# One 32 KB run per partition for K and V, and a softmax per head: a decode layer on one core

## The chip, the cores and the metric

The kernel runs on one core of a Trainium2 chip. The metric is the device time of one execution in microseconds (us), as the median of several runs. An execution has a *span*, from the first to the last instruction of the profile, and a little time around it. The engines are PE (matmuls; PEld is its loading of weights), DVE (vector work), ACT (activations), POOL (general work) and SP (which here only issues transfers). Sixteen DMA engines move data between HBM and the on-chip SBUF. PE writes its results to PSUM, eight banks of 2 KB in each partition.

## The reference

One decode step of a layer that mixes two branches with a gate. Eight batches, one new token each, width 576. Branch A is attention with 32 query heads over 16 K/V heads of 128, over the last 2048 of 8192 cached positions; branch B is an MLP of width 4608.

```python
W = min(4096, max(256, Sk // 4))                     # 2048
q = (x @ wq).reshape(B, Sq, Hq, Dh).transpose(0, 2, 1, 3)
k = jnp.repeat(k_cache[:, :, Sk - W:, :], rep, axis=1)   # rep = 2
v = jnp.repeat(v_cache[:, :, Sk - W:, :], rep, axis=1)
scores = jnp.einsum("bhqd,bhkd->bhqk", q, k) * (Dh ** -0.5)
p = _softmax(scores, axis=-1)
o = jnp.einsum("bhqk,bhkd->bhqd", p, v)
a = o.transpose(0, 2, 1, 3).reshape(B, Sq, Hq * Dh) @ wo
b = _gelu(_layernorm(x) @ w1 + b1) @ w2 + b2
g = _sigmoid((x * gate_w).sum(-1, keepdims=True))
return g * a + (1 - g) * b
```

All tensors are bf16. One K/V head of all batches is 8 x 2048 x 128 x 2 bytes = 4 MB of K and as much of V, so K and V are 134 MB of the 154 MB that are moved.

## The kernel before

**Transfers.** SP issues nearly all of them, in one order: wq and w1 first, then a stream of items, then w2. `K i` and `V i` are the 4 MB of head i; `W` is a quarter of wo, after each fourth V. The stream is K0, K1, K2, V0, K3, V1, K4, and so on: K runs three heads ahead of V. K and V go through four slots of 64 KB in each partition, taken in turn, so an item takes the slot of the item four places before it. SP waits until that slot is free: for a K item when its four transposes are done, for a V item when its PV matmuls are done. A load is cut into 256 runs of 16 KB (32 key blocks of 64 keys, by 8 batches); a partition holds two of them, of two batches.

**K.** A head is four *halves* (two units, i = 2 head + u, of two halves each). For each half DVE transposes 128x2048 words (`tr`, line 647, about 2.3 us) into one of two KT buffers, and PE multiplies it in eight matmuls of 512 columns (`qk`, line 659 for the first of four and line 175 for the three that keep the weights). The transposes of a KT buffer wait for the `qk` two halves earlier. The scores of two heads (a *group*, eight halves) add up in PSUM banks 0 to 3; a mask written into the banks beforehand keeps the parts that a partition doesn't own out of the maximum.

**Softmax of a group.** In this order: `mx` (DVE, line 620) takes the maximum over the 2048 scores of each partition; `mq`, a small matmul on PE and `nb` (lines 621 to 623) combine the partitions; `exp` (ACT, line 624) writes P and its sums; `mask` (ACT, line 629) fills the banks for the next group, and the first `qk` of that group waits for it; `pt` (DVE, line 631) transposes P into one of two buffers; a small matmul adds the sums (line 633) and `rc` (line 635) inverts them. POOL copies the queries of the next group into place in four instructions (line 614).

**V.** `pv` (PE, line 681) is 32 matmuls a head: 16 key steps, two column tiles of 32 columns side by side. After the second head of a group come `vmul` and `acc` (DVE, lines 691 and 694), `ew` (POOL, line 696), `us` (PE, line 700), `oev` (ACT, line 703), and after four heads `oT` (DVE, line 706); then a projection adds the product with that quarter of wo to a PSUM bank (line 563). The products with w2 are added to the same bank at the end.

**Order.** A planner goes through all the operations with a cost for each, a transfer rate of 428 GB/s and 1.8 us of latency, and takes, among those whose predecessors are placed, the one that can start first, a priority counting 0.2 us a step (the softmax has priority 5, mask 4, `vmul` to `us` 6, `oev` and `oT` 9, `tr`, `qk` and `pv` 0):

```python
est = max(eng_free[op.eng], r)
key = (est - 0.2 * op.prio, -op.prio, i)
```

What comes out is a fixed order on each engine; on the chip an instruction waits only for those that it depends on and for those ahead of it on its engine. Ties go to the operation that was added first, in the order of the stream.

Of the kernel before, what the change touches and what calls it, by code (L numbers as in the profile page):

```python
# [181 lines left out]
def build_kernel(nc, A_x, A_k_cache, A_v_cache, A_wq, A_wo, B_x, B_w1, B_b1, B_w2, B_b2, gate_w, out):  # L182
# [9 lines left out]
    HG = 2  # L192
    NG = Hkv // HG
    ND = 4
    SE = 4 * W
# [14 lines left out]
    with ExitStack() as es:  # L210
# [19 lines left out]
        req("i32", 32, F32)  # L230
        req("iqm", 32, F32)
        req("maskr", 4, F32)
        req("maskq", 4, F32)
        req("maskv", 4, F32)
        req("kq", 128, F32)
        req("selv", 128, F32)
        req("seln", 128, F32)
# [10 lines left out]
        req("qbd", 4 * 4 * 128, BF)  # L248
# [7 lines left out]
        req("sm", 32 * NG, F32)  # L256
        req("gcol", 1, F32)
        req("rr", 2, F32)
# [3 lines left out]
        req("oT", NG * 128, BF)  # L262
# [41 lines left out]
        i32 = view("i32")  # L304
# [3 lines left out]
        iqm, maskr, selv = view("iqm"), view("maskr"), view("selv")  # L308
# [7 lines left out]
        qbd = view("qbd").rearrange("p (u h m) -> p u h m", u=4, h=4)  # L316
# [13 lines left out]
        oT = view("oT").rearrange("p (i j c) -> p i j c", i=NG // 2, j=WOR)  # L330
        seln = view("seln")
# [53 lines left out]
        o_mR = add("pool", lambda e: e.affine_select(out=maskR, in_=ones_bf, pattern=[[0, 128], [1, 4]], compare_op=ALU.is_equal,  # L385
                                                     fill=0.0, base=0, channel_multiplier=-1), deps=[o_ones], name="maskR", cost=0.8, prio=-1)
        o_mL = add("pool", lambda e: e.affine_select(out=maskL, in_=zeros_bf, pattern=[[0, 16], [1, 4], [0, 2]], compare_op=ALU.is_equal,
# [70 lines left out]
        o_i32 = [add("dve", lambda e: e.tensor_reduce(out=i32, in_=ident.rearrange("p (q m) -> p m q", q=4), axis=AXL.X, op=ALU.add), deps=[o_ident, o_obl], name="i32", cost=0.3, prio=-1)]  # L458
        o_iqm = add("dve", lambda e: e.tensor_reduce(out=iqm.rearrange("p (q m) -> p q m", q=4), in_=ident.rearrange("p (q r m) -> p q m r", q=4, r=4), axis=AXL.X, op=ALU.add), deps=[o_ident, o_obl], name="iqm", cost=0.3, prio=-1)
        o_maskr = add("dve", lambda e: e.tensor_reduce(out=maskr, in_=i32.rearrange("p (r m) -> p r m", r=4), axis=AXL.X, op=ALU.add), deps=o_i32, name="maskr", cost=0.2, prio=-1)  # L460
        o_maskq = add("dve", lambda e: e.tensor_reduce(out=maskq, in_=ident.rearrange("p (q m) -> p q m", q=4), axis=AXL.X, op=ALU.add), deps=[o_ident, o_xT], name="maskq", cost=0.3)
        o_kq = add("pool", lambda e: e.tensor_copy(kq.rearrange("p (q m) -> p q m", q=4), bass.AP(arena_f, offset=foffs("i32"), ap=[[AST // 2, 128], [0, 4], [1, 32]])), deps=o_i32, name="kq", cost=0.3, prio=-1)
        o_maskhd = add("dve", lambda e: e.tensor_reduce(out=maskhd, in_=iqm.rearrange("p (n h) -> p h n", h=2), axis=AXL.X, op=ALU.add), deps=[o_iqm], name="maskhd", cost=0.2, prio=-1)

        def seln_fn(e):
            dst = bass.AP(arena_f, offset=foffs("seln"), ap=[[AST // 2, 128], [32, 4], [8, 4], [1, 8]])
            src = bass.AP(arena_f, offset=foffs("i32"), ap=[[AST // 2, 128], [8, 4], [0, 4], [1, 8]])
            return e.tensor_copy(dst, src)
        o_seln = [add("pool", seln_fn, deps=o_i32, name="seln", cost=0.3, prio=-1)]
        o_selv = []  # L470
        for l in range(4):
            def selv_fn(e, l=l):
                dst = bass.AP(arena_f, offset=foffs("selv") + 32 * l, ap=[[AST // 2, 128], [1, 2], [8, 4], [2, 4]])
                s0, s1 = [bass.AP(arena_f, offset=foffs("iqm") + 16 * (l % 2) + h, ap=[[AST // 2, 128], [8, 2], [0, 4], [2, 4]]) for h in range(2)]
                return e.tensor_tensor(out=dst, in0=s0, in1=s1, op=ALU.add)
            o_selv.append(add("pool", selv_fn, deps=[o_iqm], name="selv%d" % l, cost=0.3, prio=-1))
# [39 lines left out]
        for he in range(4):  # L516
            for u in range(2):
                def fn(e, he=he, u=u):
                    src = bass.AP(ps, offset=BK_SEL * 512 + 8 * he + u, ap=[[PST, 128], [64, 16], [2, 4], [32, 2]])
                    return e.activation(out=q4[:, he, :].rearrange("p (l u b h) -> p l u b h", l=16, u=2, b=4)[:, :, u, :, :], in_=src, func=ACTF.Copy)  # L520
                o_q4.append(add("act", fn, deps=[o_selp], name="q4_%d_%d" % (he, u), cost=0.3))
# [78 lines left out]
        def load_item(cache, nm, hkv):  # L600
            s = take_slot()
            src = cache[:, hkv, S0:Sk, :].rearrange("b (x r) d -> x b (r d)", x=32)
            d = dma("sp", lambda e: e.dma_start(slot(s).rearrange("p (u n) -> p u n", u=2), src), "s%d" % s, 8 * W * Dh * 2, deps=slot_free[s], name="%s%d" % (nm, hkv), after=last_dma[-1:])
            last_dma.append(d)
            slot_free[s] = []
            return s, d

        def query(g):
            qb_done[g] = []
            for a in range(4):  # L610
                def fn(e, a=a):
                    dst = bass.AP(arena, offset=32 * a * AST + aoffs("qbd") + 32 * a, ap=[[AST, 32], [520, 4], [128, 4], [1, 8]])
                    src = bass.AP(arena, offset=32 * a * AST + aoffs("q4") + 32 * g, ap=[[AST, 32], [8, 4], [256, 4], [1, 8]])
                    return e.tensor_copy(dst, src)  # L614
                qb_done[g].append(add("pool", fn, deps=o_q4 + [o_qz, qk_unit.get(4 * g - 1)], name="qr%d_%d" % (g, a), cost=0.4))

        def softmax(g):
            k = lambda i, n=1, parts=128, p0=0: sm[p0:p0 + parts, g, i:i + n]
            MX, MXQ, NB, S = 0, 1, 7, 12
            mx = add("dve", lambda e: e.tensor_reduce(out=k(MX), in_=ps[:, 0:4, :].rearrange("p a n -> p (a n)"), axis=AXL.X, op=ALU.max), deps=[qk_unit[4 * g + 3]], name="mx%d" % g, cost=2.25, prio=5)  # L620
            mq = add("dve", lambda e: e.tensor_scalar(out=k(MXQ, 4), in0=maskq, scalar1=k(MX), scalar2=-SCALE, op0=ALU.mult, op1=ALU.mult), deps=[mx, o_maskq], name="mq%d" % g, cost=0.16, prio=5)
            gp = add("pe", lambda e: e.matmul(ps[:, BK_S, 4:8], kq, k(MXQ, 4), start=True, stop=True), deps=[mq, o_kq, o_u] + b6_r[-1:], after=b6_w[-1:], name="max_pe%d" % g, cost=0.5, prio=5)  # L622
            nb = add("dve", lambda e: e.tensor_reduce(out=k(NB), in_=ps[:, BK_S, 4:8], axis=AXL.X, op=ALU.min), deps=[gp], name="nb%d" % g, cost=0.16, prio=5)  # L623
# [3 lines left out]
            if g + 1 < NG:  # L627
                query(g + 1)
                mask_done[g + 1] = add("act", lambda e: e.activation(out=ps[:, 0:4, :].rearrange("p a (n c) -> p (a n) c", c=4), in_=bass.AP(arena_f, offset=foffs("maskv"), ap=[[AST // 2, 128], [0, 512], [1, 4]]), func=ACTF.Copy),  # L629
                                       deps=[ex] + qb_done[g + 1], name="mask%d" % (g + 1), cost=1.75, prio=4)  # L630
            pt_done[g] = add("dve", lambda e: e.transpose(bass.AP(arena, offset=aoffs("PT") + 2048 * (g % 2), ap=[[AST, 128], [8, 64], [512, 4], [1, 8]]), Pm.rearrange("p (r q m) -> p r q m", q=4, m=8)),  # L631
                             deps=[ex] + ([pv_last[g - 2]] if g >= 2 else [o_yTp, o_hT]), name="pt%d" % g, cost=2.4, prio=5)
            sp_ = add("pe", lambda e: e.matmul(ps[:, BK_S, 0:1], seln, k(S), start=True, stop=True), deps=[mask_done.get(g + 1, ex)] + o_seln, after=[gp], name="sum_pe%d" % g, cost=0.5, prio=5)  # L633
            b6_w.append(sp_)
            rc = add("dve", lambda e: e.reciprocal(out=rr[:, g % 2:g % 2 + 1], in_=ps[:, BK_S, 0:1]), deps=[sp_], name="rc_%d" % g, cost=0.16, prio=5)  # L635
# [3 lines left out]
        def k_unit(i, s, d):  # L639
            g, q = divmod(i, 4)  # L640
            ub = q
            trs = []
            for h in range(2):
# [4 lines left out]
                                                                         bass.AP(arena_f, offset=foffs("RAW") + s * SE + (q % 2) * (SE // 2) + 32 * h, ap=[[AST // 2, 128], [64, 64], [1, 32]])))(),  # L648
# [4 lines left out]
                def qk_fn(e, h=h, kb=kb):  # L653
                    mm = None
                    for ee in range(2):
                        for rc in range(4):
                            rhs = bass.AP(arena, offset=aoffs("KT") + kb * 4096 + rc * 1024 + ee, ap=[[AST, 128], [2, 512]])
                            args = (ps[:, rc, :], qbd[:, ub, 2 * h + ee, :], rhs)
# [9 lines left out]
            if q == 3:  # L668
                softmax(g)

        def v_item(hkv):
            s, d = load_item(A_v_cache, "dv", hkv)
            i = 2 * hkv + 1
            g, q = divmod(i, 4)
# [159 lines left out]
```

## Time and profile before

The median is 365.9 us (three runs, 365.89 to 366.47). The profiled execution has a span of 364.9 us.

| what | number |
|---|---|
| span of the profiled execution | 364.9 us |
| median of the runs | 365.9 us |
| mean granted TensorE clock | 0.846 |
| PE busy | 247.1 us (68%) |
| DVE busy | 217.0 us (59%) |
| ACT busy | 39.9 us (11%) |
| POOL busy | 23.3 us (6%) |
| moved | 154.47 MB in 10674 packets, mean 423 GB/s |
| K load, issue to landing | 28.1 us (median of 16) |
| V load, issue to landing | 33.0 us (median of 16) |

How to read the lines of the profile: in the list of groups a line has the source line, the engine, the operation, destination and source with their shapes, the count, then busy time in us and the mean of one in ns, then the engine's idle time ahead of these instructions and what ended most of it. In the view of instructions in order of time a line begins with its start in us from the start of the span and its length; the bracket at the end is the idle time of the engine before it and what ended that. The two rows of digits give the granted clock and the busy share of the DMA engines in tenths, in 40 equal slices of the span. The list of waits has the engine, the line that waited, what it waited for, and the sum in us, the number of times and the longest. The chain is the path of work that ended last, followed back from the last instruction.

### The profile page before, as it was taken

What the parts mean: (1) busy time and instruction counts of PE and PEld (TensorE: products, weight loads), DVE (VectorE), ACT (ScalarE), POOL (GpSimd) and SP (SyncE); (2) the same over time, 40 slices, a digit from 0 to 9 for tenths busy, and PEclk for the clock granted to TensorE, in tenths of its full rate; (3) what the DMA queues carried; (4) which work ended last, traced back from release to release, by engine and by line L of the source; (5) the groups of instructions that cost most, each with busy time, mean ns of one, the idle gap of its engine ahead of it and who ended that gap; (6) DMA issues with size and microseconds to landing.
All of it is one profiled execution on the core that took longest, in us unless ns stands there. A gap on an engine that the chain in (4) does not pass through costs nothing.

```text
span 364.9 us, 2626 instructions
## 1 busy us (share of the span) xinstructions
PE 247.1 (68%) x1347; PEld 57.3 (16%) x893; DVE 217.0 (59%) x160; ACT 39.9 (11%) x46; POOL 23.3 (6%) x66
## 2 busy tenths in 40 slices
PE   0355676599486957849297957868396938587776
PEld 0100000122111121202111121202110210102333
DVE  0723999667883757256675657276756667085220
ACT  1012100400310040000400040000400040001100
POOL 7210001000100000001000100001000100000000
PEclk9986599699769986969768986989589968969699
DMA  8999999999999999999999999999999999999996
GB/s 347 432 408 429 431 433 427 408 429 432 429 431 431 436 427 431 433 431 433 428 431 433 424 433 429 431 435 431 433 429 433 433 431 429 431 431 431 426 428 263
DMA packets 10674, 154.47 MB, mean 423 GB/s; under 512 B 764, under 2 KB 932, under 8 KB 1320
## 3 DMA queue, kind: packets, MB, share of 16 engines
q1 hardware_dynamic: 10608, 154.29, 99.1%
q8 instruction: 8, 0.13, 0.1%
q10 hardware_dynamic: 56, 0.03, 0.0%
q14 instruction: 2, 0.02, 0.0%
HBM read 154.31 MB, written 0.01 MB: 423 GB/s over the span
## 4 chain that ended last, share of the span: by engine, by line
DMA 66%; DVE 21%; PE 10%; issue 1%; ACT 1%; SPq 0%; DVEq 0%
DMA arena<-in_A_k_cache_dram 59%; DVE arena L647 20%; DMA arena<-in_B_w_dram 7%; PE ps L175 5%; PE ps L659 2%; PE ps L681 2%; DVE arena L546 1%; DVE arena L620 1%; ACT ps L629 1%; PE ps L563 0%; DVE arena L545 0%; PE ps L633 0%; DVE arena L777 0%; PE ps L622 0%; SPq L406 0%
## 5 line engine op out<-in xcount | busy, mean ns | idle before, releaser
L647 DVE STREAM_TRANSPOSE arena<-arena 128x2048 f32<-128x2048 f32 x64 | 144.1, 2289 | 61.8 <-DMA arena<-in_A_k_cache_dram 40.6
L175 PE MATMUL ps<-arena 128*128 128x512 bf16 (+2 forms) x454 | 135.0, 449 | 0.0
L659 PE MATMUL ps<-arena 128*128 128x512 bf16 x128 | 57.7, 451 | 52.5 <-DVE arena L647 52.5
L681 PE MATMUL ps<-arena 128*32 128x512 bf16 x512 | 60.3, 390 | 2.6 <-DVE arena L635 1.9
L624 ACT ACTIVATE arena<-ps,arena 128x2048 bf16<-128x2048 f32 x8 | 15.7, 1967 | 240.5 <-DVE arena L623 240.5
L659 PEld LDWEIGHTS ps<-arena 128*128 128x128 bf16 x128 | 14.0, 109 | 171.9 <-DVE arena L647 114.6
L681 PEld LDWEIGHTS ps<-arena 128*32 128x32 bf16 x512 | 25.2, 99 | 46.1 <-issue 20.3
L620 DVE TENSOR_REDUCE arena<-ps 128x1 f32<-128x2048 f32 x8 | 18.3, 2287 | 12.5 <-PE ps L175 12.4
L614 POOL COPY arena<-arena 32x128 bf16<-32x128 bf16 x32 | 9.2, 288 | 211.3 <-PE ps L175 201.5
L631 DVE STREAM_TRANSPOSE arena<-arena 128x2048 bf16<-128x2048 bf16 x8 | 18.3, 2292 | 6.4 <-ACT arena L624 6.4
L691 DVE SCALAR_TENSOR_TENSOR arena<-ps,arena 128x512 f32<-128x512 f32 x8 | 6.0, 751 | 19.8 <-PE ps L681 19.8
L563 PE MATMUL ps<-arena 128*8 128x288 bf16 (+1 forms) x140 | 12.6, 339 | 6.9 <-DVE arena L706 5.6
L700 PE MATMUL ps<-arena 128*128 128x256 f32 x16 | 5.8, 444 | 16.0 <-POOL arena L696 16.0
L633 PE MATMUL ps<-arena 128*128 128x1 f32 x16 | 4.6, 359 | 15.0 <-ACT ps L629 14.2
L629 ACT ACTIVATE ps<-arena 128x2048 f32<-128x2048 f32 x7 | 13.1, 1876 | 0.1
L696 POOL TENSOR_TENSOR arena<-arena 128x256 f32<-128x256 f32 x8 | 4.9, 612 | 111.3 <-DVE arena L623 63.3
L438 PE MATMUL ps<-arena 8*128 8x8 bf16 x8 | 0.6, 171 | 14.7 <-DVE arena L412 9.6
L694 DVE TENSOR_REDUCE arena<-arena 128x128 f32<-128x512 f32 x8 | 8.4, 1048 | 0.3
L563 PEld LDWEIGHTS ps<-arena 128*8 128x8 bf16 (+1 forms) x140 | 6.4, 97 | 13.5 <-DVE arena L706 7.0
L703 ACT ACTIVATE arena<-ps,arena 64x256 bf16<-64x256 f32 x8 | 3.7, 465 | 43.1 <-PE ps L700 43.1
L706 DVE STREAM_TRANSPOSE arena<-arena 128x256 bf16<-128x256 bf16 x4 | 2.5, 634 | 9.8 <-ACT arena L703 9.8
L541 DVE TENSOR_TENSOR arena<-arena 128x1152 f32<-128x1152 f32 x1 | 1.4, 1359 | 10.5 <-ACT arena L539 10.5
(88 smaller groups left out, 66.2 us busy)
## 6 DMA issues: line engine op xcount, KB each, us to landing
arena<-in_A_k_cache_dram SPq DMA_DIRECT2D x16, 4096.0 KB, 28.1
arena<-in_A_v_cache_dram SPq DMA_DIRECT2D x16, 4096.0 KB, 33.0
arena<-in_B_w_dram SPq DMA_DIRECT2D x1, 4608.0 KB, 23.4
arena<-in_A_wo_dram SPq DMA_DIRECT2D x4, 1152.0 KB, 34.7
arena<-in_A_wq_dram SPq DMA_DIRECT2D x1, 4096.0 KB, 13.0
arena<-in_B_w_dram SPq DMA_DIRECT2D x2, 1728.0 KB, 27.3
arena<-in_B_w_dram SPq DMA_DIRECT2D x1, 1152.0 KB, 26.7
arena<-in_B_w_dram SPq DMA_DIRECT2D x1, 576.0 KB, 24.3
```

What stands on the lines that cost most here:

```text
L175: return e.add_instruction(mybir.InstMatmult(name=nc.get_next_instruction_name(), engine=mybir.EngineType.PE, ins=[e.lower_ap(rhs), e.lowe ...
L563: ins = e.matmul(ps[32 * j:32 * j + 8, BK_ACC, 0:JN], lhsT, rhs[:, JN * j:JN * j + JN], start=False, stop=True, skip_group_check=True, til ...
L614: return e.tensor_copy(dst, src)
L620: mx = add("dve", lambda e: e.tensor_reduce(out=k(MX), in_=ps[:, 0:4, :].rearrange("p a n -> p (a n)"), axis=AXL.X, op=ALU.max), deps=[qk_ ...
L624: ex = add("act", lambda e: e.activation(out=Pm, in_=ps[:, 0:4, :].rearrange("p a n -> p (a n)"), func=ACTF.Exp, bias=k(NB), scale=SCALE, ...
L629: mask_done[g + 1] = add("act", lambda e: e.activation(out=ps[:, 0:4, :].rearrange("p a (n c) -> p (a n) c", c=4), in_=bass.AP(arena_f, of ...
L631: pt_done[g] = add("dve", lambda e: e.transpose(bass.AP(arena, offset=aoffs("PT") + 2048 * (g % 2), ap=[[AST, 128], [8, 64], [512, 4], [1, ...
L647: tr = add("dve", (lambda h=h, kb=kb: lambda e: e.transpose(bass.AP(arena_f, offset=foffs("KT") + kb * 2048, ap=[[AST // 2, 128], [1, 2048]]),
L659: mm = e.matmul(*args, start=False, stop=True, skip_group_check=True) if rc == 0 else held_matmul(nc, e, *args, stop=True, skip=True)
L681: mm = e.matmul(ps[c:c + 32, BK_OS[g % 2], :], PT[:, g % 2, 16 * c + 32 * t:16 * c + 32 * t + 32], slot(s)[:, (j % 2) * SE + 512 * t:(j % ...
L691: vmul = add("dve", lambda e: e.scalar_tensor_tensor(out=vmv, in0=ps[:, BK_OS[g % 2], :].rearrange("p (r d) -> p r d", r=4), scalar=rr[:, ...
L694: acc_ev[g] = add("dve", lambda e: e.tensor_reduce(out=EV[:, g % 2, :], in_=vm.rearrange("p (r d) -> p d r", r=4), axis=AXL.X, op=ALU.add) ...
```

## The change

A K or V load becomes 128 runs of 32 KB (16 key blocks of 128 keys, by 8 batches): a partition holds one run, of one batch. With all eight batches in the partitions of a head, a group is now one head: four halves, then mx, exp, mask, pt and the rest, 16 times and not 8. `pv` uses two column tiles of 64 columns for 32. `vmul` to `oev` run for each head; `oT` stays at every fourth head. Queries have two buffers, so the query copies of head g wait for the last `qk` of head g - 2. The mask patterns go by 8 columns for 4, and their setup takes fewer instructions. K runs two heads ahead: K0, K1, V0, K2, V1, K3 and so on. The planner's costs change for some operations: `pv` 3.6 to 4.0, `vmul` 0.65 to 0.75, `acc` 0.65 to 1.05, `us` 0.7 to 0.9, `oev` 0.35 to 0.45, `oT` 0.4 to 0.65.

```diff
-    HG = 2
-    NG = Hkv // HG
+    NG = Hkv
...
-        req("qbd", 4 * 4 * 128, BF)
+        req("qbd", 2 * 2 * 4 * 128, BF)
...
-        stream = [("K", 0), ("K", 1), ("K", 2)]
+        KA = 2
+        stream = [("K", i) for i in range(KA)]
...
-            if vi + 3 < Hkv:
-                stream.append(("K", vi + 3))
+            if vi + KA < Hkv:
+                stream.append(("K", vi + KA))
...
-            src = cache[:, hkv, S0:Sk, :].rearrange("b (x r) d -> x b (r d)", x=32)
-            d = dma("sp", lambda e: e.dma_start(slot(s).rearrange("p (u n) -> p u n", u=2), src), "s%d" % s, 8 * W * Dh * 2, deps=slot_free[s], ...
+            src = cache[:, hkv, S0:Sk, :].rearrange("b (x r) d -> x b (r d)", x=16)
+            d = dma("sp", lambda e: e.dma_start(slot(s), src), "s%d" % s, 8 * W * Dh * 2, deps=slot_free[s], ...
...
-                    dst = bass.AP(arena, offset=32 * a * AST + aoffs("qbd") + 32 * a, ap=[[AST, 32], [520, 4], [128, 4], [1, 8]])
+                    dst = bass.AP(arena, offset=32 * a * AST + aoffs("qbd") + 1024 * (g % 2) + 32 * a, ap=[[AST, 32], [528, 2], [128, 4], [1, 16]])
...
-                qb_done[g].append(add("pool", fn, deps=o_q4 + [o_qz, qk_unit.get(4 * g - 1)], name="qr%d_%d" % (g, a), cost=0.4))
+                qb_done[g].append(add("pool", fn, deps=o_q4 + [o_qz, qk_unit.get(2 * g - 3)], name="qr%d_%d" % (g, a), cost=0.4))
...
-            mx = add("dve", lambda e: e.tensor_reduce(out=k(MX), in_=ps[:, 0:4, :]..., axis=AXL.X, op=ALU.max), deps=[qk_unit[4 * g + 3]], ...
+            mx = add("dve", lambda e: e.tensor_reduce(out=k(MX), in_=ps[:, 0:4, :]..., axis=AXL.X, op=ALU.max), deps=[qk_unit[2 * g + 1]], ...
...
-            g, q = divmod(i, 4)
-            ub = q
+            g, q = divmod(i, 2)
...
-            if q == 3:
+            if q == 1:
                 softmax(g)
...
-                    for j in (i - 1, i):
-                        c = 32 * (j % 4)
-                        mm = e.matmul(ps[c:c + 32, BK_OS[g % 2], :], PT[:, g % 2, 16 * c + 32 * t:16 * c + 32 * t + 32], slot(s)[:, (j % 2) * SE + 512 * t:(j % 2) * SE + 512 * t + 512],
-                                      start=(t == 0), stop=(t == 15), skip_group_check=True, tile_position=(0, c))
+                    for j in range(2):
+                        mm = e.matmul(ps[64 * j:64 * j + 64, BK_OS[g % 2], :], PT[:, g % 2, 1024 * j + 64 * t:1024 * j + 64 * t + 64], slot(s)[:, SE * j + 512 * t:SE * j + 512 * t + 512],
+                                      start=(t == 0), stop=(t == 15), skip_group_check=True, tile_position=(0, 64 * j))
...
-            prev = add("pe", pv_fn, deps=deps, name="pv%d" % i, cost=3.6, after=pv_hist[-1:])
+            prev = add("pe", pv_fn, deps=deps, name="pv%d" % g, cost=4.0, after=pv_hist[-1:])
...
-            if q == 3:
-                pv_last[g] = prev
...
+            pv_last[g] = prev
```

The operations from `vmul` to `oT` stood under that last `if` and now run for every head.

More of the change, by code (lines that the diff above doesn't have):

```diff
@@ L470, in build_kernel @@
[L470 to L476, printed above, removed]
+        o_i16 = add("dve", lambda e: e.tensor_reduce(out=i16, in_=ident.rearrange("p (q m) -> p m q", q=8), axis=AXL.X, op=ALU.add), deps=[o_ident, o_obl], name="i16", cost=0.3, prio=-1)
@@ L516, in build_kernel, with fn @@
         for he in range(4):
[L517 to L521, printed above, removed]
+            def fn(e, he=he):
+                src = bass.AP(ps, offset=BK_SEL * 512 + 8 * he, ap=[[PST, 128], [64, 16], [1, 8], [32, 2]])
+                return e.activation(out=q4[:, he, :].rearrange("p (l b h) -> p l b h", l=16, b=8), in_=src, func=ACTF.Copy)
+            o_q4.append(add("act", fn, deps=[o_selp], name="q4_%d" % he, cost=0.4))
         def h_fn(e):
@@ L621, in softmax @@
[L621 to L623 removed]
+            MX, MXQ, NB, S = 0, 1, 9, 10
@@ new lines, in v_item @@
+            pre = [keep_warm("warm0", 5, [prev])] if g == NG - 1 else []
+            u_sum[g] = add("pe", lambda e: e.matmul(ps[:, BK_OS[g % 2], 0:256], selv, EW[:, g % 2, :, :].rearrange("p h d -> p (h d)"), start=True, stop=True),
+                           deps=[ew_done[g]] + o_selv, name="us%d" % g, cost=0.9, prio=6, after=pre)
+            r0 = 32 * (g % 4)
+            o_item_ev[g] = add("act", lambda e: e.activation(out=on[r0:r0 + 32, :], in_=ps[r0:r0 + 32, BK_OS[g % 2], 0:256], func=ACTF.Copy, scale=gcol[r0:r0 + 32, :]),
+                               deps=[u_sum[g], o_gcol, oT_done.get(g // 4 - 1)], name="oev%d" % g, cost=0.45, prio=9)
@@ L710, in keep_warm @@
+            if g % 4 == 3:
+                oT_done[g // 4] = add("dve", lambda e: e.transpose(bass.AP(arena, offset=aoffs("oT") + 256 * (g // 4), ap=[[AST, 128], [1, 256]]),
+                                                                   bass.AP(arena, offset=aoffs("on"), ap=[[AST, 128], [1, WOR], [WOR, 32]])),
+                                      deps=[o_item_ev[x] for x in range(g - 3, g + 1)], name="oT%d" % (g // 4), cost=0.65, prio=9)
         def keep_warm(name, n, after):
```

100 lines of the change are left out of this document (42 added, 58 removed).

## The prediction

> **What bounds the kernel now.** Views in this order: the page's slices and chain, the list of waits of the DMA queue's issuing engine, then the instructions in order of time around the first two softmaxes. The page first:
>
> ```profile
> PEclk9986599699769986969768986989589968969699
> DMA  8999999999999999999999999999999999999996
> DMA 66%; DVE 21%; PE 10%; issue 1%; ACT 1%; SPq 0%; DVEq 0%
> L647 DVE STREAM_TRANSPOSE arena<-arena 128x2048 f32<-128x2048 f32 x64 | 144.1, 2289 | 61.8 <-DMA arena<-in_A_k_cache_dram 40.6
> ```
>
> The transfers are busy in every slice but the ends, and DMA has 66% of the chain; DVE, with the most work beside PE, is idle 40.6 us for K. So the transfers set the time: a stretch of 295 us in the middle ran at 430 GB/s. Four heads of K and V and one piece of wo are 8 x 4.194 + 1.18 = 34.7 MB, 80.8 us at that rate: **20.2 us a head**. Compute fits under that as long as a head needs less. The waits of the issuing engine say that the slots come free well before the transfers need them:
>
> ```profile
> SPq L603 <- DVE arena L647: 212.4, 15, 17.8
> SPq L603 <- PE ps L681: 25.9, 8, 5.0
> ```
>
> These waits cost nothing now, because a K load still takes 28.1 us from issue to landing, some 18 of it behind loads issued earlier. What the compute chain needs if nothing waits for data can be read early in the run, where K0 to K2 have landed and the chain runs freely from the first softmax (60.71) to the second (93.86):
>
> ```profile
> 45.22 15.56 DVE L647 STREAM_TRANSPOSE arena<-arena 128x2048 f32<-128x2048 f32 x7
> 58.58 0.40 PE L659 MATMUL ps<-arena 128*128 128x512 bf16 x1 [0.22 <-DVE arena L647]
> 60.71 2.25 DVE L620 TENSOR_REDUCE arena<-ps 128x1 f32<-128x2048 f32 x1
> 63.28 0.39 PE L622 MATMUL ps<-arena 128*128 128x4 f32 x2 [2.73 <-DVE arena L621]
> 63.90 1.97 ACT L624 ACTIVATE arena<-ps,arena 128x2048 bf16<-128x2048 f32 x1 [25.51 <-DVE arena L623]
> 65.99 1.88 ACT L629 ACTIVATE ps<-arena 128x2048 f32<-128x2048 f32 x1
> 66.01 2.29 DVE L631 STREAM_TRANSPOSE arena<-arena 128x2048 bf16<-128x2048 bf16 x1
> 67.92 0.59 PE L633 MATMUL ps<-arena 128*128 128x1 f32 x2 [4.26 <-ACT ps L629]
> 68.37 0.59 PE L659 MATMUL ps<-arena 128*128 128x512 bf16 x1
> 71.75 0.63 PE L659 MATMUL ps<-arena 128*128 128x512 bf16 x1
> 73.97 3.63 PE L681 MATMUL ps<-arena 128*32 128x512 bf16 x32
> 77.54 0.40 PE L659 MATMUL ps<-arena 128*128 128x512 bf16 x1
> ...
> 91.84 0.40 PE L659 MATMUL ps<-arena 128*128 128x512 bf16 x1
> 91.96 0.75 DVE L691 SCALAR_TENSOR_TENSOR arena<-ps,arena 128x512 f32<-128x512 f32 x1 [3.44 <-PE ps L681]
> 92.74 1.07 DVE L694 TENSOR_REDUCE arena<-arena 128x128 f32<-128x512 f32 x1
> 93.86 2.29 DVE L620 TENSOR_REDUCE arena<-ps 128x1 f32<-128x2048 f32 x1
> 93.89 0.61 POOL L696 TENSOR_TENSOR arena<-arena 128x256 f32<-128x256 f32 x1 [31.94 <-DVE arena L694]
> 94.56 0.70 PE L700 MATMUL ps<-arena 128*128 128x256 f32 x2 [0.74 <-POOL arena L696]
> ```
>
> Scores (qk), max (mx), exp and mask share PSUM banks 0 to 3, so they are one serial chain: from mx at 60.71 to the next qk at 68.37 PE waits for mx, nb, exp and mask. That is 7.66 us (7.91 at the second softmax, 93.86 to 101.77). Two heads take 93.86 - 60.71 = 33.15 us, 16.6 a head, under 20.2. This is the slack that the change spends.
>
> **Part by part.**
>
> *Larger runs.* In the packet records of the trace a 16 KB packet takes 611 ns, a 32 KB one (wq) 1213: 9 ns less than two. A load has 16 packets on each of 16 engines now, 8 after; 8 x 9 ns x 32 loads = **2.3 us less**, if the transfers still bound. Bounds: 0, and 3 (the fastest 16 KB packet is 609). For a loss by the new addresses no row speaks; I leave it to the rivals.
>
> *K two ahead.* V0 and K2 swap places, and K15 comes one load (9.7 us) later. Head i's V still lands three loads after its K, and a slot comes round after four loads, so each has about 29 us. K0's transposes end near 49.7 and its slot is wanted by V1 near 66. Nothing, by the cover of that slack.
>
> *Setup.* Four copies on ACT for eight, and fewer POOL and DVE masks: a few 0.2 to 0.3 us instructions, all before K0 lands at 37.3, behind that load. Nothing; uncovered, under 1 us gained.
>
> *Softmax per head.* Sixteen chains for eight. Added eight times: on DVE mx 2.29, mq 0.23, nb 0.16, the transpose of P 2.29, the reciprocal 0.17, vmul 0.75, acc 1.05, in all 6.9 us; on ACT exp 2.1, mask 1.9, oev 0.47; on PE two small products (0.4 and 0.6) and us (0.7); on POOL four query copies (1.33) and ew 0.61. DVE's 55 us bring it to 272 of 365, which would fit; POOL's and ACT's too (query copies are two heads early). They aren't the price. The price is that the serial chain is now paid per head, on PE's order.
>
> That order is fixed by the planner, which takes what can start first, a priority counting 0.2 us a step. I worked it through by hand with its own costs. After mx: the max product, nb, exp, mask, the sum product, qk0, qk1. Then qk2 must wait for its transpose, which starts only after qk0 has freed a KT buffer (2.3 us against qk1's 1.95), so PV of the head just finished, ready by then, starts about 0.5 us sooner and goes **between qk1 and qk2**. That is where it ran at 73.97. Then qk2, then us, whose priority puts it ahead of qk3 though PE must idle for it, then qk3, then the next mx. In the planner's costs a head takes 7.55 + 3.90 + 4.0 + 1.95 + 0.77 + 0.9 + 1.95 + 0.08 = 21.1 us against 20.3 for its transfers, so V always waits for PV, and this order repeats for each head.
>
> In the rows of the chip, mx to next mx:
> - mx to qk0: 7.66 and 7.91, take 7.8
> - qk0 and qk1: 68.37 to 73.97 is 5.60, at the second softmax 101.77 to 107.75 is 5.98; take 5.8. These are at half clock (a warm half takes 1.82).
> - PV: 73.97 to 77.54, 3.57. Its stationary tiles widen from 32 to 64 columns, a case that no row has. Bounds: 3.57 (same count, same 512 columns, two side by side) and 7.2 (one after the other, 32 x 0.226, from 0.90 us for four qk matmuls). Nearest is today's row: two tiles, two column positions. 3.6.
> - end of PV to us: 91.84 to 94.56, 2.7, with qk2 (1.8) beneath it
> - us: 0.5, of 0.70 with its pipeline
> - qk3 to mx: 58.58 to 60.71, 2.1
>
> Sum **22.5 us a head**, over 20.2. The 2.3 us of the packets is then worth nothing; late next is PE at qk0, and SP's issues wait for slots: K of head i+2 is queued behind transposes of head i, V and wo behind it, but each lands a head early.
>
> The sum: the first mx starts when the third of the seven transposes from 45.22 ends, 51.9. Fifteen periods give 337.5. After the sixteenth mx: 7.7 to PV (3.2 to exp, 2.1 to the transpose, 2.3), PV 4.7 (3.6 warm, 5.8 at half clock at 341.03), 4.6 to the end of oT (351.1 to 355.7), 2.0 for 16 projection matmuls (135.37), 1.9 to the end (363.0 to 364.9): 20.9. The W2 transfers end before that. Span 410; the profiled execution has span 364.9 beside a median of 365.9, 1.0 more, so **411 us**, 12% slower.
>
> [...] In this trace every softmax gap on PE is followed by a granted clock of 0.50 (100 to 105 us, 180 to 185, 220 to 225), at the first two with an idle stretch of only 4.26 us, and a qk half then takes 3.38 instead of 1.82. [...]
>
> **Rivals.**
> [...]
> - *Transfers still bound; faster.* PV falls under mx instead of between qk1 and qk2, as at 330.87, where it ran in the 3.5 us between the last qk and the max product. The period is then 22.5 - 3.6 = 18.9, under 20.2, and the transfers decide. 365.9 - 2.3, plus 0 to 2 because K15 lands 9.7 us later (its softmax takes 22.5 us from landing to the end of its transpose, so PV of head 15 starts 3 to 5 us after V15): **364.5**. It decides wherever a head stays below 20.2. For: late V in the paced groups do this. Against: V now lands before its P is ready.
> - *PV tiles don't run side by side*, or cold lasts through PV: a period of 24.5 to 26, **442** to 464. Against: 3.57 for 32 matmuls today. Transfers that the new addresses slow down would have to lose 10% before the chain notices.
>
> **How the numbers follow.** Chain as worked out 0.73, at 411, own range 398 to 426 (cold 1.7 to 3.4 us a head, planner's PV 4.0 for 3.6). PE warm 0.09. Transfers bound 0.10: 0.08 faster, 0.02 within 0.2% (about what a measurement of this kernel tells from no change). Overlap lost or colder 0.08. So 0.08, 0.02, 0.90, and a range of 386 to 430.
>
> **What would show it.** Right: 16 max reduces about 22.5 us apart; PV between second and third qk of the next head; the chain mostly PE, DVE and ACT; DMA slices of 8 or 9 with about 378 GB/s over the span; longer waits of SP on the transposes; packets near 6,600; PV's 32 matmuls in 3.6 us. Wrong: DMA at 9 throughout and spacing near 20, where the order or the clock is not as worked out; PV at 7 us; us behind qk3 (1.4 us a head less).

## The result and the profile after

The changed kernel takes **700.0 us** (median of 4 executions, 699.4 to 701.5) against 366.0 us for the kernel before in the same series: a ratio of 1.913, with a 95% interval of 1.911 to 1.916. The forecast was 411, with a range of 386 to 430. The sign was right and the cause was not.

The page of the changed kernel, span 699.4 us: granted clock, busy share of the DMA engines and GB/s in 40 slices, then the chain that ended last, DVE's transposes of K, and the DMA issues with KB each and us from issue to landing.

```profile
PEclk9957575956767595676767595776758557685869
DMA  9999999999999999999999999999999999999991
GB/s 385 310 211 212 212 209 214 213 217 210 214 229 209 217 216 216 210 215 223 219 218 235 216 218 212 214 217 212 212 206 240 214 213 212 210 211 210 212 356 43
...
another core or an unknown queue 35%; PE 30%; DVE 13%; issue 10%; DMA 6%; ACT 5%; SPq 0%; POOL 0%; DVEq 0%; POOLq 0%
...
L631 DVE STREAM_TRANSPOSE arena<-arena 128x2048 f32<-128x2048 f32 x64 | 146.6, 2302 | 250.4 <-DMA arena<-in_A_k_cache_dram 200.7
...
arena<-in_A_k_cache_dram SPq DMA_DIRECT2D x16, 4096.0 KB, 62.1
arena<-in_A_v_cache_dram SPq DMA_DIRECT2D x16, 4096.0 KB, 74.1
...
arena<-in_A_wq_dram SPq DMA_DIRECT2D x1, 4096.0 KB, 13.3
```

The row to read is GB/s. It starts at 385 while wq arrives, falls to about 212 as soon as K and V follow, stays between 206 and 240 for the rest of their loads, and is back at 356 for the last weights. The row of the DMA's busy share stays at 9 all the way: the engines are as busy as before and move half as much. DVE waited 40.6 us for K before; it waits 200.7 now. The transposes themselves last what they did (2302 ns, 2289 before). The chain doesn't show the cause: it gives DMA 6% and leaves 35% to an unknown queue.

In the packet records of the trace a 32 KB packet of K or V lasts 2524 ns (median). One of wq, of the same size in the same run, lasts 1213, and a 16 KB packet of K or V lasted 611 before. A load of 4.194 MB at 212 GB/s is 19.8 us, two of them 39.6 us a head; before it was 9.75. For 32 loads that is 322 of the 334 us lost. (In the packet records K and V take 644.8 us from first to last, and 321.4 before.)

The spacing of the max reduces says the same. The view of one source line (count, ns of the shortest, median and longest, first and last start):

```profile
L605 DVE TENSOR_REDUCE arena<-ps x16: 2247/2252/2291, 69.9 to 662.9; 128x1 f32<-128x2048 f32 x16
```

(662.9 - 69.9) / 15 = 39.5 us a head, about two loads. One head in order of time (start, length; in brackets PE's or DVE's idle time and what ended it):

```profile
117.71 0.59 PE L643 MATMUL ps<-arena 128*128 128x512 bf16 x1
...
121.03 0.39 PE L643 MATMUL ps<-arena 128*128 128x512 bf16 x1
...
127.50 5.33 PE L663 MATMUL ps<-arena 128*64 128x512 bf16 x32 [4.51 <-DMA arena<-in_A_v_cache_dram]
...
132.77 0.40 PE L643 MATMUL ps<-arena 128*128 128x512 bf16 x1
...
135.48 0.70 PE L681 MATMUL ps<-arena 128*128 128x256 f32 x2 [0.73 <-POOL arena L677]
136.01 0.39 PE L643 MATMUL ps<-arena 128*128 128x512 bf16 x1
...
147.37 2.31 DVE L631 STREAM_TRANSPOSE arena<-arena 128x2048 f32<-128x2048 f32 x1 [12.64 <-DMA arena<-in_A_k_cache_dram]
149.61 2.25 DVE L605 TENSOR_REDUCE arena<-ps 128x1 f32<-128x2048 f32 x1
```

PE's order is the one worked out ahead: qk0, qk1, PV, qk2, us, qk3. But PV waits for V, and 12.64 us of DVE's idle time ends with the next K. The waits of the issuing engine (sum in us, times, longest) grew, as forecast, for a reason that was not:

```profile
SPq L588 <- DVE arena L631: 477.6, 15, 36.5
SPq L588 <- PE ps L663: 82.0, 13, 7.1
```

Queue time is the effect here and not the cause: each slot is held longer since the data comes later. (A slot is 32 KB in each partition; the description of the kernel before calls it 64 KB.)

The rest of the loss, some 11 us, lies behind the last load: from its last packet to the end of the span it is 29.1 us, and 17.9 before. PE's order for the end of the run is fixed too:

```profile
662.93 2.29 DVE L605 TENSOR_REDUCE arena<-ps 128x1 f32<-128x2048 f32 x1 [3.28 <-PE ps L175]
...
678.12 2.90 PE L547 MATMUL ps<-arena 128*8 128x288 bf16 x24 [3.32 <-DMA arena<-in_B_w_dram]
...
680.95 0.39 PE L607 MATMUL ps<-arena 128*128 128x8 f32 x2
```

The products with w2 (L547) stand ahead of the last max product (L607), and w2 is issued behind all of K and V. So the last softmax waits: the max product starts 18.0 us after its max reduce. With the same order and the transfers of before, in the first experiment below, it starts 2.6 us after it (384.92 to 387.53).

### The profile page after: what moved, and what is told of

Same layout as the page of the kernel before. It is cut to its first block, busy times and chain, and to the rows that moved or that the text cites. A ratio compares the mean times of both kernels' runs of the same rounds, so it can differ in the third digit from the quotient of the medians.

```text
span 699.4 us, 2915 instructions
## 1 busy us (share of the span) xinstructions
PE 298.5 (43%) x1395; PEld 81.0 (12%) x941; DVE 272.4 (39%) x216; ACT 75.4 (11%) x74; POOL 35.9 (5%) x102
## 2 busy tenths in 40 slices
DMA packets 6581, 154.50 MB, mean 221 GB/s; under 512 B 764, under 2 KB 932, under 8 KB 1320
## 4 chain that ended last, share of the span: by engine, by line
another core or an unknown queue 35%; PE 30%; DVE 13%; issue 10%; DMA 6%; ACT 5%; SPq 0%; POOL 0%; DVEq 0%; POOLq 0%
PE ps L663 12%; PE ps L175 11%; DMA arena<-in_A_k_cache_dram 6%; DVE arena L631 6%; DVE arena L605 4%; PE ps L643 4%; ACT ps L614 4%; PE ps L607 1%; PE ps L618 1%; PE ps L547 1%; ACT arena L609 1%; DVE arena L606 0%; DVE arena L608 0%; DVE arena L530 0%
## 5 line engine op out<-in xcount | busy, mean ns | idle before, releaser
L631 DVE STREAM_TRANSPOSE arena<-arena 128x2048 f32<-128x2048 f32 x64 | 146.6, 2302 | 250.4 <-DMA arena<-in_A_k_cache_dram 200.7
L663 PE MATMUL ps<-arena 128*64 128x512 bf16 x512 | 88.0, 520 | 57.4 <-DMA arena<-in_A_v_cache_dram 57.4
L607 PE MATMUL ps<-arena 128*128 128x8 f32 x32 | 9.3, 365 | 163.2 <-DVE arena L606 163.2
L609 ACT ACTIVATE arena<-ps,arena 128x2048 bf16<-128x2048 f32 x16 | 31.5, 1967 | 290.8 <-DVE arena L608 290.8
L663 PEld LDWEIGHTS ps<-arena 128*64 128x64 bf16 x512 | 37.1, 147 | 119.9 <-DMA arena<-in_A_v_cache_dram 76.5
L547 PE MATMUL ps<-arena 128*8 128x288 bf16 (+1 forms) x140 | 15.4, 385 | 63.0 <-DVE arena L687 48.5
L616 DVE STREAM_TRANSPOSE arena<-arena 128x2048 bf16<-128x2048 bf16 x16 | 36.7, 2296 | 2.1 <-ACT arena L609 2.1
L605 DVE TENSOR_REDUCE arena<-ps 128x1 f32<-128x2048 f32 x16 | 36.1, 2254 | 3.3 <-PE ps L175 3.3
L607 PEld LDWEIGHTS ps<-arena 128*128 128x128 f32 x32 | 7.8, 304 | 179.4 <-DVE arena L606 179.1
L614 ACT ACTIVATE ps<-arena 128x2048 f32<-128x2048 f32 x15 | 28.2, 1880 | 0.5
L599 POOL COPY arena<-arena 32x128 bf16<-32x128 bf16 x64 | 18.3, 286 | 79.9 <-PE ps L175 67.7
L675 DVE TENSOR_REDUCE arena<-arena 128x128 f32<-128x512 f32 x16 | 17.0, 1063 | 0.5
L547 PEld LDWEIGHTS ps<-arena 128*8 128x8 bf16 (+1 forms) x140 | 7.1, 107 | 76.0 <-DVE arena L687 52.3
L618 PEld LDWEIGHTS ps<-arena 128*128 128x128 f32 x32 | 7.8, 304 | 67.8 <-ACT ps L614 65.3
```

Of the source, the lines that this page charges most:

```text
L547: ins = e.matmul(ps[32 * j:32 * j + 8, BK_ACC, 0:JN], lhsT, rhs[:, JN * j:JN * j + JN], start=False, stop=True, skip_group_check=True, til ...
L607: gp = add("pe", lambda e: e.matmul(ps[:, BK_S, 8:16], kq, k(MXQ, 8), start=True, stop=True), deps=[mq, o_kq, o_u] + b6_r[-1:], after=b6_w ...
L609: ex = add("act", lambda e: e.activation(out=Pm, in_=ps[:, 0:4, :].rearrange("p a n -> p (a n)"), func=ACTF.Exp, bias=k(NB), scale=SCALE, ...
L618: sp_ = add("pe", lambda e: e.matmul(ps[:, BK_S, 0:1], kq, k(S), start=True, stop=True), deps=[mask_done.get(g + 1, ex)], after=[gp], name ...
L631: tr = add("dve", (lambda h=h, kb=kb: lambda e: e.transpose(bass.AP(arena_f, offset=foffs("KT") + kb * 2048, ap=[[AST // 2, 128], [1, 2048]]),
L663: mm = e.matmul(ps[64 * j:64 * j + 64, BK_OS[g % 2], :], PT[:, g % 2, 1024 * j + 64 * t:1024 * j + 64 * t + 64], slot(s)[:, SE * j + 512 * ...
```

## The experiments

Two questions come first: does the compute chain cost what the prediction worked out, and are the transfers slow by themselves? Then, why they are slow. Windows below have the stretch, its length, the busy us of PE, PEld, DVE, ACT and POOL with their counts, the granted clock, the DMA share and GB/s.

**The changed compute with the transfers of before, and the reverse.** The edit of the first, in the changed kernel; the second makes the opposite edit in the kernel before:

```diff
-            src = cache[:, hkv, S0:Sk, :].rearrange("b (x r) d -> x b (r d)", x=16)
-            d = dma("sp", lambda e: e.dma_start(slot(s), src), ...
+            src = cache[:, hkv, S0:Sk, :].rearrange("b (x r) d -> x b (r d)", x=32)
+            d = dma("sp", lambda e: e.dma_start(slot(s).rearrange("p (u n) -> p u n", u=2), src), ...
```

> The changed kernel's compute, in its own order, with the transfers of before (256 runs of 16 KB, 32 key blocks by 8 batches, two runs in a partition). K and V therefore lie in other partitions than the masks and sums assume; the work and its order are those of the changed kernel. Theory (the addresses alone made the transfers slow, and the chain per head is the second bound, as the prediction worked out): transfers at 430 GB/s again, max reduces about 22.5 us apart, 405 to 420 us. Rival (the chain per head is hidden too): transfers bound, 363 to 368 us. Rival (the slow part is in the compute, which holds the slots): near 700 us.

> The kernel before with the changed kernel's transfers alone (128 runs of 32 KB, 16 key blocks by 8 batches, one run in a partition), so its masks assume another layout than K and V have. Theory (addresses alone): K and V at about 212 GB/s, 19.6 us a load, near 690 us, all but a per cent of the changed kernel's time. Rival (the new compute is needed for the slow-down): 364 to 368 us.

The first takes 407.1 us, ratio 1.112 (1.108 to 1.115); the second 693.5 us, ratio 1.893 (1.887 to 1.899). The changed compute with the old transfers: the max reduces, then one head in order of time.

```profile
L605 DVE TENSOR_REDUCE arena<-ps x16: 2252/2292/2293, 52.0 to 384.9; 128x1 f32<-128x2048 f32 x16
```

```profile
207.44 2.29 DVE L605 TENSOR_REDUCE arena<-ps 128x1 f32<-128x2048 f32 x1 [0.85 <-PE ps L175]
...
214.70 0.59 PE L618 MATMUL ps<-arena 128*128 128x1 f32 x2 [4.26 <-ACT ps L614]
...
215.15 0.59 PE L643 MATMUL ps<-arena 128*128 128x512 bf16 x1
...
218.35 0.39 PE L643 MATMUL ps<-arena 128*128 128x512 bf16 x1
...
220.24 3.64 PE L663 MATMUL ps<-arena 128*64 128x512 bf16 x32
...
223.82 0.40 PE L643 MATMUL ps<-arena 128*128 128x512 bf16 x1
...
226.52 0.70 PE L681 MATMUL ps<-arena 128*128 128x256 f32 x2 [0.73 <-POOL arena L677]
227.06 0.39 PE L643 MATMUL ps<-arena 128*128 128x512 bf16 x1
...
229.06 2.29 DVE L605 TENSOR_REDUCE arena<-ps 128x1 f32<-128x2048 f32 x1 [0.34 <-PE ps L175]
```

The first max reduce starts at 52.0 (51.9 expected), and (384.9 - 52.0) / 15 = 22.2 us a head (22.5 expected). The head shown takes 21.6, as every second one does, and the heads between take 22.7. The parts stand nearly as they were summed: 7.7 to qk0, a cold qk0 of 3.2 us behind an idle stretch of 4.26, PV with 64-column tiles in 3.64 for 32 matmuls (so two tiles do run side by side; one after the other they were put at 7.2), 2.7 from the end of PV to us, 2.0 from qk3 to the next max.

The kernel before with the new transfers, its middle:

```profile
50.00:640.00 590.00, 253.95 (x1050) 52.97 (x665) 195.73 (x118) 29.92 (x27) 11.68 (x34) 0.69 1.01 214
```

So the transfers alone make the loss, whatever compute stands beside them: 327.3 us (693.5 less the 366.2 of the same series), where the whole change lost 334. The chain works as forecast; in the changed kernel it is hidden under loads that take twice as long.

**Is it the length of the run?** Each load as two transfers with runs of 16 KB, to the same places:

```diff
+            src = cache[:, hkv, S0:Sk, :].rearrange("b (x h r) d -> h x b (r d)", x=16, h=2)
+            for h in range(2):
+                d = dma("sp", ... e.dma_start(slot(s)[:, SE * h:SE * h + SE], src[h]) ...
```

> The changed kernel, each load cut in two transfers that bring the first and the second 16 KB of every partition: runs of 16 KB, the same places, the same two batches under way at a time. Theory (which addresses are read at the same time): still slow, 16 KB packets of about 1250 ns for 611, 650 to 700 us. Rival (the length of a run from a strided source): packets near 611 ns and 405 to 420 us.

685.6 us, ratio 1.871 (1.864 to 1.878).

```profile
50.00:620.00 570.00, 247.76 (x1062) 64.37 (x701) 238.28 (x165) 61.67 (x56) 24.62 (x70) 0.69 1.01 221
```

A 16 KB packet now takes 1225 ns, where the kernel before has 611. The length is not it.

**Do the eight batches, far apart in memory, collide?** Eight transfers a load, one batch each: 16 rows of 32 KB into every eighth partition.

```diff
+            for b in range(8):
+                src = cache[b, hkv, S0:Sk, :].rearrange("(x r) d -> x (r d)", x=16)
+                d = dma("sp", ... e.dma_start(bass.AP(arena, offset=b * AST + aoffs("RAW") + s * DE, ap=[[8 * AST, 16], [1, DE]]), src) ...
```

> The changed kernel, each load cut in eight transfers, one for each batch, of 16 runs of 32 KB (a run for every DMA engine) into every eighth partition. The same layout in SBUF and the same run of 32 KB; what differs is that all engines read one batch at a time. Theory (batches read at the same time collide): 32 KB packets near 1213 ns, transfers at 430 GB/s, and the chain per head bounds: 405 to 420 us. Rival (32 KB pitch between the engines is what collides): packets stay near 2500 ns, about 700 us. Rival (chain hidden): 363 to 368 us.

705.0 us, ratio 1.924 (1.919 to 1.928), packets of 2526 ns, 214 GB/s in the middle. That theory falls.

**Is it the distance between the runs?** In the kernel before, four patterns of four heads each: one contiguous 4 MB; the layer's runs with a pitch of 36 KB; eight heads of one batch; a pitch of 48 KB.

```diff
+                # contiguous
+                    return cache[hkv % 8].rearrange("h s d -> (h s d)")[o:o + 128 * DE].rearrange("(p n) -> p n", p=128)
+                # eight heads of one batch
+                    return cache[hkv % 8, h0:h0 + 8, S0:Sk, :].rearrange("h (x r) d -> x h (r d)", x=16)
+                # 16 runs with a pitch of `kind` keys of 256 bytes
+                return cache[:, hkv, Sk - 16 * kind:Sk, :].rearrange("b (x r) d -> x b r d", x=16)[:, :, 0:128, :].rearrange("x b r d -> x b (r d)")
```

> The kernel before; every K and V load is 128 runs of 32 KB, with another source for each four heads, so what it computes isn't the layer; the rate of each stretch is what is read. Heads 0 to 3: one contiguous piece of 4 MB of one batch. Heads 4 to 7: 16 runs 36 KB apart, by 8 batches. Heads 8 to 11: 16 runs 32 KB apart, by 8 heads of one batch (2 MB apart, not 33.5 MB). Heads 12 to 15: 16 runs 48 KB apart, by 8 batches. Theory A (streams whose addresses differ by multiples of 32 KB within a small region collide): stretch 2 and 4 at 430 GB/s, stretch 3 at 212, stretch 1 fast as wq was, or slow if only wq's uneven start saved it. Theory B (the 33.5 MB between batches): stretches 1 and 3 at 430, 2 and 4 at 212.

One execution, a window in each of the four stretches:

```profile
35.00:80.00 45.00, 29.54 (x128) 4.67 (x60) 38.44 (x23) 5.68 (x5) 1.16 (x4) 0.82 1.00 431
180.00:230.00 50.00, 19.36 (x74) 3.23 (x43) 13.88 (x7) 0.00 (x0) 0.00 (x0) 0.67 1.01 212
340.00:410.00 70.00, 25.65 (x104) 4.13 (x58) 20.66 (x10) 0.00 (x0) 1.15 (x4) 0.70 1.00 211
525.00:580.00 55.00, 23.79 (x101) 5.10 (x70) 12.44 (x7) 0.00 (x0) 0.00 (x0) 0.72 1.00 210
```

Contiguous data in 32 KB runs arrives at 431 GB/s. All others stay at half: other pitches, and another distance in place of that of the batches. Four more pitches gave the same:

> As the run with four patterns, all with 8 batches and runs of 32 KB; heads 0 to 3 have 64 KB from run to run, heads 4 to 7 128 KB, heads 8 to 11 33 KB, heads 12 to 15 32.25 KB. Theory A (multiples of 32 KB collide): the first two at 212 GB/s or less (128 KB perhaps half of that), 33 KB between 212 and 430, 32.25 KB near 212. Theory B (batches 33.5 MB apart collide): all four at 212.

64, 128, 33 and 32.25 KB, again in one execution: 213, 214, 214 and 212 GB/s.

**The two halves of a partition from places 256 KB apart** (a pitch of 16 KB in each transfer, as before had):

```diff
-            src = cache[:, hkv, S0:Sk, :].rearrange("b (x h r) d -> h x b (r d)", x=16, h=2)
+            src = cache[:, hkv, S0:Sk, :].rearrange("b (h x r) d -> h x b (r d)", x=16, h=2)
```

> The changed kernel with its layout of 16 key blocks by 8 batches in the partitions, but a partition holds two runs of 16 KB that lie 256 KB apart, brought by two transfers, so that the 16 blocks of a transfer lie 16 KB apart and not 32 KB. The keys of a head are in another order, the same for K and V. Theory A (the 32 KB pitch): 430 GB/s, and the chain per head bounds, 403 to 415 us. Theory B (batches): still near 212 GB/s, about 690 us.

679.4 us, ratio 1.857 (1.852 to 1.861), 223 GB/s. No pitch that was tried matters.

The same kernel with PV held back until behind the next head's max product, as a repair of the chain:

```diff
-            prev = add("pe", pv_fn, ..., after=pv_hist[-1:])
+            prev = add("pe", pv_fn, ..., after=pv_hist[-1:] + gp_of[g + 1:g + 2])
```

> The run with two runs of 16 KB in a partition, and PV of a head placed behind the max product of the next head (in PE's idle time for exp and mask) and no longer between its second and third qk. If the chain per head is what the 407 us were made of: the max reduces come down from 22.2 us to 20.2 (the transfers' pace), and 364 to 372 us. If it is not PV's place but the added softmax work itself that bounds: 395 to 410 us.

669.8 us, ratio 1.835 (1.829 to 1.841). With the transfers still slow this says nothing of the chain; it is made again below. Its executions scatter from 662 to 675, and why its transfers run at 225 GB/s and not at 223 was not followed up.

**Is it the shape that the source has?** What all slow transfers share is a source (for each batch or all of them) whose outermost size is 16. In the kernel before, again four patterns: 32 outer rows by 4 batches; 16 outer rows of 256 KB with gaps of 4 KB, so nearly contiguous; the eight transfers by batch of above, but into 16 neighbouring partitions each; 64 outer rows by 2 batches.

```diff
+                src = cache[0:nb, hkv, Sk - 128 * nx:Sk, :].rearrange("b (x r) d -> x b (r d)", x=nx)
...
+                NE = 8 * DE + 2048
+                src = cache[hkv].rearrange("h s d -> (h s d)")[0:16 * NE].rearrange("(x n) -> x n", x=16)[:, 0:8 * DE].rearrange("x (y n) -> x y n", y=8)
...
+                    d = dma("sp", ... e.dma_start(slot(s)[16 * b:16 * b + 16, :], src) ...
```

> The kernel before with runs of 32 KB from another source in each four heads, so what it computes isn't the layer; the rate of each stretch is what is read. Theory A (32 KB pitch) has fallen. [...] Theory D: the source addresses decide. [...]

One execution, a window in each stretch:

```profile
30.00:80.00 50.00, 33.36 (x175) 5.09 (x71) 38.85 (x23) 7.49 (x6) 1.15 (x4) 0.83 1.00 430
160.00:210.00 50.00, 17.55 (x84) 4.38 (x60) 13.56 (x10) 4.41 (x4) 0.61 (x1) 0.69 1.00 210
350.00:455.00 105.00, 30.70 (x131) 7.66 (x98) 20.06 (x13) 4.41 (x4) 0.61 (x1) 0.61 1.01 153
575.00:600.00 25.00, 18.56 (x90) 3.59 (x50) 16.14 (x9) 0.11 (x1) 0.00 (x0) 0.81 0.98 414
```

One property now tells all patterns apart. With the same 32 KB runs, batches as far apart and all 128 partitions written, 32 or 64 outer rows run at 430 and 414 GB/s (packets of 1213 ns), and 16 outer rows at 210 (2520 ns), though their addresses are nearly contiguous. No pattern with 16 outer rows was fast, and none with 32 or more was slow. The third line shows that the place in SBUF matters: the transfers by batch read the same sources as above, there into every eighth partition at 214 GB/s, here into 16 neighbouring ones at 153.

Why 16 outer rows halve the rate, and why 16 neighbouring partitions slow it further, no run shows: a packet record has a size and a time, not the place that was written.

**What the rest of the change would do at full speed.** The changed compute with the old transfers, and PV behind the next head's max product (the diff above):

> The changed kernel's compute with the transfers of before (as the first run), and PV of a head placed behind the max product of the next head. K and V lie in other partitions than the masks assume. If PV's place between second and third qk is what lifts the chain over the transfers' pace: max reduces 20.2 us apart on average, transfers busy throughout, 364 to 372 us. If the added softmax work itself bounds: 395 to 407 us.

369.1 us, ratio 1.0075 (1.0047 to 1.0103). The max reduces, and a window near the end:

```profile
L605 DVE TENSOR_REDUCE arena<-ps x16: 2252/2292/2293, 52.2 to 344.0; 128x1 f32<-128x2048 f32 x16
```

```profile
360.00:365.00 5.00, 5.00 (x72) 2.90 (x66) 0.64 (x1) 0.12 (x1) 0.00 (x0) 1.00 0.24 92
```

(344.0 - 52.2) / 15 = 19.5 us a head: with PV moved the chain is hidden under the transfers again. (From K0 to K15 there are 29 loads and three pieces of wo, 291 us at 430 GB/s, so 19.4 a head is the pace at which K comes.) The transfers end near 362, as in the kernel before, but PE has projection work left.

**What 32 KB runs are worth at full rate.** The kernel before with each K and V as one contiguous 4 MB:

```diff
-            src = cache[:, hkv, S0:Sk, :].rearrange("b (x r) d -> x b (r d)", x=32)
-            d = dma("sp", lambda e: e.dma_start(slot(s).rearrange("p (u n) -> p u n", u=2), src), ...
+            src = cache[hkv % 8].rearrange("h s d -> (h s d)")[o:o + 128 * DE].rearrange("(p n) -> p n", p=128)
+            d = dma("sp", lambda e: e.dma_start(slot(s), src), ...
```

> The kernel before with K and V as one contiguous piece of 4 MB a load, 128 runs of 32 KB, so half as many packets at the full rate; it isn't the layer's K and V. The prediction's packet term (9 ns saved for each pair of 16 KB packets, 8 on each engine, 32 loads): 2.3 us less than the kernel before, ratio 0.993 to 0.995. Rival: the term is hidden or not there, ratio 0.998 to 1.002.

364.6 us against 365.7, ratio 0.9959 (0.9943 to 0.9974). The middle of it, and of the kernel before:

```profile
50.00:345.00 295.00, 211.34 (x1054) 46.90 (x689) 188.75 (x117) 32.33 (x30) 12.29 (x35) 0.84 1.00 432
```

```profile
50.00:345.00 295.00, 210.38 (x1050) 46.94 (x685) 188.49 (x117) 32.34 (x30) 12.35 (x35) 0.84 1.01 430
```

So that gain is real and is 1.1 us by the medians. The source is contiguous here as well, so it isn't the length of the run alone.

**K two heads ahead, alone,** in the kernel before:

```diff
-        stream = [("K", 0), ("K", 1), ("K", 2)]
+        KA = 2
+        stream = [("K", i) for i in range(KA)]
...
-            if vi + 3 < Hkv:
-                stream.append(("K", vi + 3))
+            if vi + KA < Hkv:
+                stream.append(("K", vi + KA))
```

> The kernel before with K two heads ahead and nothing else. The prediction costs this step at nothing, by slack of the slots: ratio 0.998 to 1.002. Rival: a group of two heads needs the third K, and the transfers stall: over 1.01.

374.0 us, ratio 1.020 (1.017 to 1.024). The max reduces of the kernel before, then of this one, then DVE ahead of this one's last K, then three windows at its end:

```profile
L620 DVE TENSOR_REDUCE arena<-ps x8: 2253/2292/2292, 60.7 to 331.0; 128x1 f32<-128x2048 f32 x8
```

```profile
L621 DVE TENSOR_REDUCE arena<-ps x8: 2291/2292/2293, 60.8 to 345.0; 128x1 f32<-128x2048 f32 x8
```

```profile
330.69 0.75 DVE L692 SCALAR_TENSOR_TENSOR arena<-ps,arena 128x512 f32<-128x512 f32 x1 [5.63 <-PE ps L682]
331.47 1.04 DVE L695 TENSOR_REDUCE arena<-arena 128x128 f32<-128x512 f32 x1
332.44 4.49 DVE L648 STREAM_TRANSPOSE arena<-arena 128x2048 f32<-128x2048 f32 x2
```

```profile
355.00:360.00 5.00, 5.00 (x42) 2.01 (x39) 0.00 (x0) 0.00 (x0) 0.00 (x0) 0.63 0.98 412
360.00:365.00 5.00, 3.56 (x25) 1.05 (x17) 1.80 (x2) 0.00 (x0) 0.61 (x1) 1.00 0.21 80
365.00:374.00 9.00, 7.08 (x97) 3.98 (x93) 1.10 (x2) 0.87 (x2) 0.00 (x0) 1.00 0.01 3
```

The transfers still run at full rate until about 361. But the last group can begin only when K15 is there, one load later: by the packet records near 326, and near 317 before. It then waits some 6 us more, since its transposes stand on DVE behind `vmul` and `acc`, and these wait for PV; in the kernel before they start as K15 lands (318.41). So the max reduce starts 14 us later, the softmax and two PVs run into the end of the transfers, and 9 us of the span stand behind them, 7 of them busy on PE.

## Why the prediction was wrong, step by step

- **Larger runs** is the step that failed. It priced only the time per packet, at 2.3 us less, and left a loss by the new addresses to a rival's last sentence ("would have to lose 10% before the chain notices"), with no price, chance or place in the range. They lost half: 611 ns for 16 KB became 2524 for 32 KB, 212 GB/s for 430, 322 us. The bounds of that step were 0 and 3 us less. The row it went by, wq's 32 KB packets at 1213 ns, is evidence for the length of a run; the new transfer differs from the old one in the count of its outer rows as well, 16 for 32. The packet term itself was right in sign and about twice too large: 1.1 us for 2.3.
- **Softmax per head** was right in mechanism and in size: order on PE, cold qk0, PV at 3.6, 22.2 us a head for 22.5, 407.1 us in all for 411 with the old transfers. In every second head qk1 comes warm, at 1.89 us (218.35 to 220.24) for 2.79 (240.14 to 242.93), so that qk0 and qk1 take 5.1 there (215.15 to 220.24) and 6.1 between (236.77 to 242.93), 5.6 on average and not 5.8. Fifteen periods of 22.2 are 4.6 us less than the sum, and the stretch from the last max reduce to the end is 19.4 (384.9 to 404.3) for 20.9. In the changed kernel the chain per head doesn't bound, so the forecast of 411 named a cost that is hidden.
- **K two ahead**, "nothing", failed too, though this did not decide. The slots did have the slack that was claimed (its transfers still ran at 430 GB/s from 340 to 350 us); what was overlooked is that the last K, and behind it DVE's fixed order, set when the last softmax begins. Alone it costs 8.3 us (374.0 against 365.7). The prediction saw this end only within one rival, as 0 to 2 us.
- **Setup** was not measured by itself; the first max reduce at 52.0 for 51.9 leaves no room for much.
- **The rivals.** "PV tiles not side by side" falls with 3.64 us. "PE warm", with its 0.09 and the low end of the range, 386, falls with 22.2 us a head: no run shows a share of heads in which the clock holds, and what the runs showed in its place stands in the next point. "Transfers bound; faster" had the right bound for the wrong reason. With PV moved and the old transfers it is 369.1 and not faster: the chain is hidden, and the end costs 3.4 us. With the 1.1 us of larger runs at full rate it would be about 368, an estimate by subtraction.
- **The clock.** The trace agrees with the rows used: in the run with the old transfers the gaps of 4.26 us ahead of 214.70 and 236.32 left qk0 at 3.20 us (215.15 to 218.35) and 3.37 (236.77 to 240.14), for the 1.82 of a warm half. On that run's chain the start of mask and the start of PV are 7.4 to 8.6 us apart in all fourteen heads that it lists, 7.5 and 8.6 in these two.
- **What would show it.** Several signs named as "right" came although the account was wrong: PE's order, packets near 6,600 (6,581), longer waits of SP, and a chain with little DMA in it (6%). The ones that told were the spacing, 39.5 us for 22.5, DMA at 9 throughout, which was listed as "wrong", and the GB/s row, 212 for the 378 named, which pointed at the step.

What stays open is why 16 outer rows gave 212 GB/s for 430, and why 16 neighbouring partitions gave 153. No version of the layer that is faster than the kernel before was found: its 16 key blocks of 128 keys are what makes the outer size 16.

## What to carry to other kernels

A transfer's shape can be a cost of its own, as here (210 GB/s with 16 outer rows, 430 with 32, for the same 32 KB runs): before trusting a row for one length of run, compare the outermost count of the source and of the destination too, and give a loss there a price and a chance even if no row speaks. A DMA share of 1.0 said here only that the engines were occupied (1.00 to 1.02 at 210 to 215 GB/s, 1.01 at 430); read it beside the GB/s and the time of one packet of known size. When a load is moved later in a stream, look at the end of the run as well as at the slots: what begins only with the last load?

## What was not expected of the hardware

- With 16 outer rows, 4 MB loads into all 128 partitions ran at 210 to 215 GB/s, at pitches of 32 to 128 KB, for eight batches or eight heads, and with a nearly contiguous source (221 and 223 as two transfers of 16 KB runs); with 32 rows, or contiguous over 128 partitions, at 430 to 432, and with 64 rows at 414.
- All 16 engines reported as busy at that half rate (DMA share 1.00 to 1.02); the loss stands in the time of each packet (2524 ns for 1213).
- Transfers by batch from the same sources went at 214 GB/s into every eighth partition and at 153 into 16 neighbours.
- Runs of 32 KB from a contiguous source, for 16 KB at the same full rate, are worth 0.4% of this kernel (0.9959).
